# A fused FNet and expert-layer kernel: the slots of its tile pairs in another order, and three late operand sums and four value fills in other places

## The chip, the cores and the metric

The kernel runs on one core of a Trainium2 chip. The metric is the device time of one execution in microseconds (us). A core has a matrix engine (TensorE, PE in the profile, its weight loads PEld), VectorE (DVE), ScalarE (ACT), GpSimd (POOL), and SyncE (SP), which here issues almost all DMA transfers. Every engine works through its own list of instructions in order; semaphores make one engine wait for another.

## The reference

With `x` of 2048 tokens by 512 values, the kernel computes a sum of three things:

```python
xn = layernorm(x)
a, b = xn @ dft_hid_re.T, xn @ dft_hid_im.T
fnet = dft_seq_re @ a - dft_seq_im @ b          # real part of a 2-D Fourier transform

q = xn @ w_q                                    # 32 heads, two halves of 128
s1, s2 = q1 @ k1.T, q2 @ k2.T                   # 64 scores each
top 2 of each -> 4 candidate pairs -> best 2 -> expert i1 * 64 + i2, g = softmax
peer = sum over heads and picks of g * gelu(xn . u[expert]) * v[expert]   # 4096 experts

out = x + fnet + peer
```

## The kernel before

**Precision.** Operands are held as two 16-bit parts, high and low, and a product is three matmuls: high by high, high by low, low by high.

**Stages.** The first 120 us compute the Fourier part. From about 120 to 420 us the routing stage runs: 8 chunks of heads (`j`) by 16 tiles of 128 tokens (`i`). For each of the 128 (j, i) steps, `scores` computes 12 matmuls into a PSUM bank (L252), ACT copies them to an SBUF tile `ss` (L951), and DVE finds the two best values and their places (L955, L959). After a chunk, `routing` turns the picks into experts and gates (L884 to L924): parts on POOL, parts on DVE, one exponential on ACT (L892). The last chunk's routing runs on DVE alone. Into the same 128 steps a table `todo` hangs extra work, one list of functions per step: `fill_load` and `fill_uv` load 512 KB of `u` or `v` and split it (ACT L780 and L781, then POOL L782); `sum_x(b, ...)` forms, for one pair of token tiles, the four sums of operand blocks that the pairs need later (POOL L822 to L831), splits them (ACT L794, POOL L795) and stores them to DRAM (`t_d`, SP L798). `sum_x` and the fills share SBUF: the sums of pair b=8 are formed in the space of `v` tiles 5 and 6, those of b=10 in that of 7 and 8, and those of b=12 again in 5 and 6, so that these four `v` tiles can be filled only when the sums in them are out. These fills are the last four of the list `fills`.

**The dense stage.** From 420 us every token tile is multiplied with all 4096 experts (z), the result goes through a gelu, is multiplied by the gates (a comparison on DVE and matmuls L1252 give them), and is multiplied with `v` (L1297). The order of the phases is z0, z1, v0, then six pairs, each followed by two v phases: z(2,3), v1, v2, z(4,5), v3, v4, and so on up to z(12,13). The pairs begin on PE at 490.6, 577.4, 666.9, 756.2, 844.3 and 933.8 us.

**A pair.** `z_pair` handles two token tiles at once. Half of the 16 expert groups are *plain tiles* (`u_part`, 24 matmuls of 256 columns, L1095, 2.62 us on PE). The other eight form two quads, `a` and `b`; each quad is computed by seven *part products* in place of eight (24 matmuls of 128 columns, L1164, 1.34 us each), from sums of operand blocks. A string `SEQ` sets the order on PE: "1a" is part product 1 of quad a, "c" a plain tile. Part products 1, 2 and 5 of a quad open a PSUM bank each (X, Y, Z); 6, 7 and 4 go on in X, and 3 in Z. After each slot, ACT or DVE takes the intermediate out: 1 and 5 and 6 and 7 by an ACT copy (L1198, L1203, L1205, L1211), 2 and 3 by a DVE addition (L1200, L1208), 7 also by L1212, with gelus (L1191) behind 6, 7 and 4. A plain tile takes one bank and ends in two gelus (L1102). There are four banks for all this, handed out first in, first out; Y is free after 2's addition, Z after 3's, X only after 4's gelu.

**Side work in a pair.** Slots of a pair that use a sum of `u` blocks (5, 6, 3, 7) read it from a ring of three SBUF buffers `s`, 512 KB each. A small planner decides which load goes behind which use (`ring_plan`); SP issues it when that use's matmuls are done (L1147). At fixed shares of the pair's time, `after` adds other units: the gate work, and checks of the Fourier inputs (`compare`), which load a 64 KB and a 448 KB piece (`cx`, L1326, L1327), reduce and subtract on DVE (L1328, L1347, L1353) and sum absolute values on ACT (L1373).

```python
SEQ = "1a 5a 2a c 6a c 3a c 7a c 1b 5b 4a 2b c 6b c 3b 7b c c 4b".split()
for n, b in zip((19, 22, 25, 107, 111, 114), PAIRS):
    todo[n].append(lambda at, b=b: sum_x(b, 0, at))
```

Within each engine the program's final order is set by a scheduler when the kernel is built, so it is not exactly the order of the code.

Of the kernel before, what the change touches and what calls it, by code (L numbers as in the profile page):

```python
# [29 lines left out]
V1 = 5  # L30
V2 = 9
QUADS = (8, 10, 12, 14), (9, 11, 13, 15)
PAIRS = tuple(range(2, 14, 2))
# [3 lines left out]
def tile_fnet_peer(ctx, tc, x, ca, cb, c5, wt, wf, wr, wq, kt, ut, vn, out):  # L37
# [683 lines left out]
    def part_b(safe, stS, stP, stQ, stE, xt, u_sb, cmp_p, w4):  # L721
# [11 lines left out]
        def behind(src, at):  # L733

            if at is None:
                return src
            nc.scalar.activation(at, src, AF.Copy)
            return at
# [48 lines left out]
        def scratch(g):  # L787
            return v_sb[g].rearrange("p l c d -> p (l c d)").bitcast(F32)

        def split4(part, t, h, dst, at):  # L790

            l = t.bitcast(F16)[:, 0:2 * D]
            if part == 0:
                nc.scalar.activation(h, t, AF.Copy, scale=behind(one, at))  # L794
                nc.gpsimd.tensor_tensor(l, t, h, op=ALU.subtract)  # L795
                return
            for i, v in enumerate((h, l)):
                nc.sync.dma_start(dst(i), v)  # L798
# [17 lines left out]
        def sum_x(b, part, at=None):  # L816

            n = (0, 2, 4, 5, 7, 5)[PAIRS.index(b)]
            f, t4 = scratch(n), scratch(n + 1)
            if part == 0:  # L820
                v = xq[b // 2]
                nc.gpsimd.tensor_copy(f[:, 0:1], behind(one, at))  # L822
                nc.gpsimd.tensor_tensor(f.rearrange("p (q f) -> p q f", q=2),  # L823
                                        v[:, :, 0].rearrange("p q k n -> p q (k n)"),
                                        v[:, :, 1].rearrange("p q k n -> p q (k n)"), op=ALU.add)
                b11, b21, b12, b22 = [f[:, k * 256:k * 256 + 256] for k in range(4)]
                r = [t4[:, k * 256:k * 256 + 256] for k in range(4)]
                nc.gpsimd.tensor_tensor(r[0], b12, b11, op=ALU.subtract)
                nc.gpsimd.tensor_tensor(r[1], b22, r[0], op=ALU.subtract)
                nc.gpsimd.tensor_tensor(r[2], b22, b12, op=ALU.subtract)  # L830
                nc.gpsimd.tensor_tensor(r[3], b21, r[1], op=ALU.subtract)  # L831
                return
            split4(part - 1, t4, f.bitcast(F16)[:, 0:2 * D],
                   lambda i: t_d[b // 2, :, i * 2 * D:i * 2 * D + 2 * D], at)
# [132 lines left out]
        todo = [[] for _ in range(NCH * NT)]  # L967
# [8 lines left out]
        else:  # L976
# [8 lines left out]
            for j in range(2, NCH):  # L985
                for t in range(4):
                    todo[(j - 1) * NT + 2 * t - (12 if j == 2 else 4)].append(
                        lambda at, j=j, t=t: m_prep(j, t, wqp, behind(sw, at)))
        fills = [divmod(n, 16) for n in (0, 1, 2, 8, 3, 10, 16, 4, 12, 14, 17, 5, 9, 11, 18, 6, 13, 15, 19, 7, 20,
                                         21, 22, 23, 24)]  # L990
        slots = [29, 31, 36, 43, 45] + [16 * j + i for j in range(3, 7) for i in (4, 6, 11, 13)]
        slots += [119 + 2 * n for n in range(len(fills) - len(slots))]
        assert fills[slots.index(119)] == (1, V1)
        for (which, g), n in zip(fills, slots):
            todo[n].append(lambda at, w=which, g=g: fill_uv(w, g, at))
            todo[n - (3 if n < 119 else 1)].append(lambda at, w=which, g=g: fill_load(w, g))
            if which == 0 and not safe and any(g in q for q in QUADS):
                todo[n + 5].append(lambda at, g=g: (sum_u(g, 1, at), sum_u(g, 2)))
        if not safe:
            for n, b in zip((19, 22, 25, 107, 111, 114), PAIRS):  # L1000
                todo[n].append(lambda at, b=b: sum_x(b, 0, at))
                todo[n + (4 if n == 114 else 5)].append(lambda at, b=b: (sum_x(b, 1, at), sum_x(b, 2)))
        for g, n in zip(range(V2, 16), (25, 38, 41, 57, 73, 89, 105)):
            todo[n].append(lambda at, g=g: stage_v(g, at, False))
            todo[n - 3].append(lambda at, g=g: fill_load(1, g))
# [98 lines left out]
        if not safe:  # L1104
            sx = stE.enter_context(tc.tile_pool(name="sx", bufs=1, side="left"))
            x4 = sx.tile([P, 2, 4, 2, P], F16, name="x4")
            PLAIN = [g for g in range(16) if not any(g in q for q in QUADS)]
            SEQ = "1a 5a 2a c 6a c 3a c 7a c 1b 5b 4a 2b c 6b c 3b 7b c c 4b".split()
            OPS = {"1": (0, None, None, 0), "2": (1, None, None, 1), "5": (None, 0, 0, None), "6": (None, 1, 1, None),
                   "3": (None, 3, None, 3), "7": (None, 2, 2, None), "4": (3, None, 3, None)}  # L1110

        USES = []
        if not safe:
            clock = 0
            for n in range(len(PAIRS)):
                for o in SEQ:
                    ns = 2616 if o == "c" else 1344
# [53 lines left out]
        def z_pair(b, n, after):  # L1171

            cgs = iter(PLAIN)
            st = {}
            total, done, cg = sum(2616 if o == "c" else 1344 for o in SEQ), 0, 0
            for o in SEQ:
                if o == "c":
# [374 lines left out]
        for ph in phases[2:]:  # L1552
            if ph[0] == "z":
                n = 4 * len(ph[1:]) - 2
# [26 lines left out]
        for n, ph in enumerate(phases):  # L1581
            if ph[0] == "z":
                b = ph[1:]
# [13 lines left out]
            b = ph[1]  # L1597
# [23 lines left out]
        return None if safe else ret  # L1621

    rs = part_b(False, stS, stP, stQ, stE, xt, u_sb, cmp_p, w4)
    stR = ExitStack()
    stR.enter_context(tc.If(rs > 0))
    r2 = nc.values_load(flag2, min_val=0, max_val=1)
    with tc.If(r2 > 0):
        MS.clear()
        stE = ExitStack()
        uvp = stE.enter_context(tc.tile_pool(name="uvp2", bufs=1, side="right"))  # L1630
        cmp_p = stE.enter_context(tc.tile_pool(name="cmpp2", bufs=1, side="right"))
        w4 = wq_space("w4p2")
        u_sb = [uvp.tile([P, 2, 2, KD, P], F16, name=f"us{g}") for g in range(16)]
        stQ = ExitStack()
        PS[0] = stQ.enter_context(tc.tile_pool(name="psum2", bufs=1, space=bass.MemoryType.PSUM))
        stP = ExitStack()
        PA[0] = stP.enter_context(tc.tile_pool(name="psa2", bufs=1, space=bass.MemoryType.PSUM))
        stS = ExitStack()
        xtp = stS.enter_context(tc.tile_pool(name="xtp2", bufs=1, side="left"))
        xt = [xb2[:, i] if i < 2 else xtp.tile([P, 2, KD, P], F16, name=f"xs{i}") for i in range(NT)]  # L1640
        for i in range(NT):
            nc.sync.dma_start(xt[i].rearrange("p a k n -> p (a k n)"), xt_d[i])
        for k in range(2):
            MP[k] = stS.enter_context(tc.tile_pool(name=f"mps{k}", bufs=1, side="left"))
        part_b(True, stS, stP, stQ, stE, xt, u_sb, cmp_p, w4)
# [3 lines left out]
    with tc.If(rv > 0):  # L1649
        with tc.tile_pool(name="gen", bufs=1) as gp, \  # L1650
# [22 lines left out]
            for q in range(4):  # L1673
                ya = gp.tile([P, 4, D], F32, tag="ya", name=f"gya{q}")
                for ri in range(2):
# [25 lines left out]
                    for a in range(4):  # L1701
                        py = pb(f"gy{q}{ri}{a}")
                        n = 0
# [9 lines left out]
                        b = 4 * a + q  # L1713
# [55 lines left out]
```

## Time and profile before

| | |
|---|---|
| median of 3 runs | 1145.59 us (1145.26 to 1149.68) |
| the profiled execution | 1145.57 us |
| its span (first to last instruction) | 1143.8 us |
| granted TensorE clock, mean | 0.996 |
| routing stage | about 120 to 420 us |
| six pairs, first to last start | 490.6 to 933.8 us |

A row of the timeline reads: start, duration, engine, line, operation, output<-input, and in brackets how long the engine had been idle and what released it. A row of the waits reads: engine and line that waited, what it waited for, then the sum in us, how often, and the longest.

### The profile page before, as it was taken

The page shows a single profiled execution, that of the slowest core. Times are in us where ns is not written, and L with a number is a line of the kernel's source. Part 1 is how long each engine was busy: PE and PEld are TensorE (multiplying, and loading weights), DVE is VectorE, ACT ScalarE, POOL GpSimd, SP SyncE. Part 2 cuts the span into 40 slices and gives each one's busy share as a digit, 9 for nine tenths or more (in the row PEclk, how much of TensorE's full clock was granted, in tenths as well). Part 3 has the DMA queues.
Part 4 walks back from the last instruction along what each step waited for, and adds up shares of the span by engine and source line. Part 5 has one row for each costly group of instructions (what it writes and reads, how often), then busy time and mean ns, then how long its engine had stood idle before and what let it go on. Part 6 is the DMA issues. An engine that isn't in the chain of part 4 may idle for free.

```text
span 1143.8 us, 27323 instructions
## 1 busy us (share of the span) xinstructions
PE 1123.1 (98%) x10748; PEld 726.1 (63%) x10748; DVE 949.7 (83%) x2855; ACT 642.1 (56%) x1086; POOL 312.3 (27%) x342
## 2 busy tenths in 40 slices
PE   9999999999999999999999999999999999999997
PEld 6455454544544469687487488479478569567763
DVE  7899979989889899956985895895996886889782
ACT  6557598788787374454444445435435534545542
POOL 1415896887888730000000000000010010000000
PEclk8999999999999999999999999999999999999999
DMA  9884455435333216453752762763663654565743
GB/s 283 278 208 162 164 167 188 140 110 194 114 134 105 75 51 207 157 210 123 259 180 101 243 222 92 229 213 119 222 206 131 219 198 145 186 235 174 237 148 105
DMA packets 114856, 198.36 MB, mean 173 GB/s; under 512 B 34068, under 2 KB 57499, under 8 KB 114718
## 3 DMA queue, kind: packets, MB, share of 16 engines
q1 hardware_dynamic: 114416, 196.45, 51.5%
q8 instruction: 86, 1.41, 0.5%
q14 instruction: 52, 0.43, 0.1%
q10 hardware_dynamic: 302, 0.08, 0.1%
HBM read 165.75 MB, written 24.97 MB: 167 GB/s over the span
## 4 chain that ended last, share of the span: by engine, by line
PE 50%; DVE 7%; DMA 5%; POOL 2%; ACT 2%; issue 1%; SPq 0%; ACTq 0%; POOLq 0%; DVEq 0%
PE v L1297 24%; PE z L1095 14%; PE z L1164 7%; DMA cx<-in_cb_dram 4%; PE g L1252 4%; PE s L252 2%; DVE L L1242 1%; DVE w L1260 1%; DVE cx L1347 1%; DVE act L1268 1%; ACT cx L1373 1%; POOL v L823 1%; DMA fit<-in_wq_dram 1%; DVE R L1247 0%; DVE R L1250 0%
## 5 line engine op out<-in xcount | busy, mean ns | idle before, releaser
L252 PE MATMUL s<-m,xq 128*128 128x512 f16 x1344 | 297.4, 379 | 2.5 <-ACT ss L951 2.5
L1297 PE MATMUL v<-v,act 128*128 128x512 f16 x1056 | 233.3, 379 | 0.0
L252 PEld LDWEIGHTS <-xq 128*128 128x128 f16 x1344 | 129.7, 98 | 153.5 <-issue 3.8
L1095 PE MATMUL z<-xb,u 128*128 128x128 f16 (+1 forms) x2688 | 219.9, 242 | 5.0 <-ACT act L1191 4.7
L1095 PEld LDWEIGHTS <-u 128*128 128x128 f16 x2688 | 196.7, 98 | 18.2 <-issue 5.6
L1310 POOL TENSOR_TENSOR y<-y,xr 128x512 f32<-128x512 f32 x15 | 24.6, 1643 | 638.8 <-DMA y<-y_d 380.5
L1242 DVE TENSOR_TENSOR L<-io_lam,cmp 128x2048 f16<-128x2048 f16 x128 | 158.4, 1237 | 41.3 <-PE g L1252 41.3
L1297 PEld LDWEIGHTS <-act 128*128 128x128 f16 x1056 | 101.2, 98 | 117.6 <-issue 0.2
L955 DVE MAX8 vals<-ss 128x8 f32<-128x64 f32 x896 | 133.4, 216 | 3.0 <-ACT ss L951 3.0
L951 ACT ACTIVATE ss<-s,wsc 128x512 f32<-128x512 f32 x120 | 81.7, 684 | 44.1 <-PE s L252 35.5
L1297 PE MATMUL v<-v,w 128*128 128x512 f16 x480 | 106.2, 379 | 0.0
L1373 ACT ACTIVATE cx<-cx 128x896 f32<-128x896 f32 x64 | 60.4, 943 | 63.5 <-DVE cx L1353 49.0
L959 DVE FIND_INDEX8 idx<-vals,ss 128x8 uint16<-128x256 f32 x224 | 93.8, 419 | 0.0
L1267 ACT ACTIVATE act<-w 128x1024 f16<-128x1024 f32 x36 | 48.4, 1360 | 69.2 <-DVE w L1260 69.0
L1297 PEld LDWEIGHTS <-w 128*128 128x128 f16 x480 | 45.9, 98 | 53.4
L1102 ACT ACTIVATE act<-z,scl 128x256 f32<-128x256 f32 (+1 forms) x88 | 44.1, 525 | 49.5 <-PE z L1095 49.5
L1252 PEld LDWEIGHTS <-L 128*128 128x128 f16 x2048 | 60.2, 96 | 12.0 <-issue 1.5
L1260 DVE SCALAR_TENSOR_TENSOR w<-act,scl,g 128x1024 f32<-128x1024 f32 x44 | 55.7, 1276 | 13.4 <-ACT act L1191 13.4
L1347 DVE TENSOR_TENSOR cx<-cx 128x512 f32<-128x512 f32 (+2 forms) x84 | 48.4, 610 | 18.6 <-DMA cx<-in_cb_dram 18.5
L1164 PEld LDWEIGHTS <-s 128*128 128x128 f16 x1080 | 62.7, 98 | 0.5
L1252 PE MATMUL g<-R,L 128*128 128x32 f16 x2048 | 62.0, 176 | 1.0 <-DVE R L1250 0.9
L1268 DVE TENSOR_TENSOR act<-w,act 128x1024 f16<-128x1024 f32 x44 | 59.2, 1348 | 2.3 <-ACT act L1267 2.3
(363 smaller groups left out, 1729.2 us busy)
## 6 DMA issues: line engine op xcount, KB each, us to landing
v<-v_d SPq DMA_DIRECT2D x67, 512.0 KB, 4.6
cx<-in_cb_dram SPq DMA_DIRECT2D x64, 448.0 KB, 5.4
s<-s_d SPq DMA_DIRECT2D x35, 512.0 KB, 4.5
w<-in_wq_dram SPq DMA_DIRECT2D x28, 512.0 KB, 6.1
fit<-in_wq_dram SPq DMA_DIRECT2D x28, 512.0 KB, 4.3
uv<-in_vn_dram SPq DMA_DIRECT2D x16, 512.0 KB, 4.0
uv<-in_ut_dram SPq DMA_DIRECT2D x16, 512.0 KB, 4.0
c<-in_ca_dram SPq DMA_DIRECT2D x8, 512.0 KB, 7.5
```

Of the source, the lines that this page charges most:

```text
L252: nc.tensor.matmul(ps, xt[i][:, l, kd, :], m[:, r, kd, :], start=(n == 0), stop=(n == 3 * KD - 1))
L951: nc.scalar.activation(s, ps, AF.Copy, scale=inv)
L955: nc.vector.max(vals[:, i, w, :, h], s[:, g, :])
L959: nc.vector.max_index(idx[:, i, w].rearrange("p k h -> p (k h)"), vals[:, i, w, 0:2].rearrange("p k h -> p (k h)"), s[:, w * HC:g + 1, :]. ...
L1095: nc.tensor.matmul(ps if n == 1 else ps.rearrange("p (b n) -> p b n", b=2), ug[:, l, c % 2, kd, :], xb2[:, k0, r, kd, :] if n == 1 else xb ...
L1164: nc.tensor.matmul(bank[:, t * P:(t + 1) * P], lt, rt, start=(t == k == 0 and op in "125"), stop=(t == 3 and k == 5), skip_group_check=op ...
L1242: nc.vector.tensor_tensor(L.rearrange("p t (l two) -> p t l two", two=2), io_lam.rearrange("p (l two) -> p l two", two=2).unsqueeze(1).to_ ...
L1252: nc.tensor.matmul(p[:, hf, t * NC:(t + 1) * NC], L[:, t, :], R[:, t, :], start=True, stop=True)
L1260: nc.vector.scalar_tensor_tensor(w, act[:, :, ts], fw, p.rearrange("p h (n c) -> p c (h n)", c=NC), op0=ALU.mult, op1=ALU.mult)
L1268: nc.vector.tensor_tensor(w16[..., 1], w, w16[..., 0], op=ALU.subtract)
L1297: nc.tensor.matmul(pv, w16[:, c, :, l], v_sb[g][:, r, cc, :], start=(n + cc == 0 and k == 0), stop=(n == 15 and cc == 1 and k == 2))
L1373: later.append(lambda: nc.scalar.activation(tf[:, P:], tf[:, P:], AF.Abs, accum_out=chk[:, n:n + 1]))
```

## The change

Three tables change; the numbers of instructions on every engine stay as they were.

```diff
         fills = [divmod(n, 16) for n in (0, 1, 2, 8, 3, 10, 16, 4, 12, 14, 17, 5, 9, 11, 18, 6, 13, 15, 19, 7, 20,
-                                         21, 22, 23, 24)]
+                                         23, 24, 21, 22)]
         slots = [29, 31, 36, 43, 45] + [16 * j + i for j in range(3, 7) for i in (4, 6, 11, 13)]
-        slots += [119 + 2 * n for n in range(len(fills) - len(slots))]
-        assert fills[slots.index(119)] == (1, V1)
+        slots += [119 + 2 * n for n in range(4)]
...
-            for n, b in zip((19, 22, 25, 107, 111, 114), PAIRS):
+            for n, b in zip((19, 22, 25, 106, 109, 118), PAIRS):
                 todo[n].append(lambda at, b=b: sum_x(b, 0, at))
-                todo[n + (4 if n == 114 else 5)].append(lambda at, b=b: (sum_x(b, 1, at), sum_x(b, 2)))
+                todo[n + (4 if n == 118 else 5)].append(lambda at, b=b: (sum_x(b, 1, at), sum_x(b, 2)))
...
-            SEQ = "1a 5a 2a c 6a c 3a c 7a c 1b 5b 4a 2b c 6b c 3b 7b c c 4b".split()
+            SEQ = "1a 5a 2a c 6a c 3a c 1b 7a 2b 5b 6b 4a c 3b c c 7b c c 4b".split()
```

The last four fills (numbers 21 to 24 are `v` tiles 5 to 8, at steps 119, 121, 123, 125) come as 7, 8, 5, 6 instead of 5, 6, 7, 8. The sums for pairs b=8, 10, 12 start at steps 106, 109, 118 instead of 107, 111, 114. In a pair the first eight slots stay; then six part products stand in a row (1b 7a 2b 5b 6b 4a), and the two plain tiles that stood among them come later. One line less in the code moves all later line numbers down by one: L1164 of before is L1163 in the change.

On POOL, at the end of the routing stage's chunk 6 (its routing ends in L924, L895, L924), this is one piece of the difference; `c`, `z`, `g`, `lc`, `di` belong to `routing`; `v_920` and `v_921` are the space of `v` tiles 5 and 6, `v_922` and `v_923` that of 7 and 8:

```order
-L795 TENSOR_TENSOR v_921<-v_921,v_920 128x1024
 L924 CAST z<-lc_0_5210 128x16x2x4 x2
+L895 TENSOR_TENSOR g_0_5272<-c_0_5163,g_0_5272 128x16x4
+L795 TENSOR_TENSOR v_923<-v_923,v_922 128x1024
 L924 CAST z<-di_0_5202 128x16x2x4 x2
-L822 COPY v_920<-ss_2_5185 128x1
+L822 COPY v_920<-ss_6_5328 128x1
 L823 TENSOR_TENSOR v_920<-xq_109 128x1024
 L828 TENSOR_TENSOR v_921<-v_920 128x256
```

The sum block of pair b=12 (L822 on) stood ahead of the gate multiplication L895 of chunk 6, and now stands behind it.

On DVE, in the middle of pair b=4 (`cx` are compare tiles; L1212, in the change L1211, is the addition behind 7a; L1200, in the change L1199, the addition behind 2b), before:

```order
L1328 TENSOR_REDUCE sums<-cx_8897 128x1
L1347 TENSOR_TENSOR cx_8897<-cx_8897 128x768
L1212 TENSOR_TENSOR w_126<-w_126,act_8248 128x4x128
L1353 TENSOR_TENSOR cx_8897<-cx_8897 128x128
L1328 TENSOR_REDUCE sums<-cx_8984 128x1
L1347 TENSOR_TENSOR cx_8984<-cx_8984 128x768
L1353 TENSOR_TENSOR cx_8984<-cx_8984 128x128
L1200 TENSOR_TENSOR act_8248<-z_4_0_8651,act_8248 128x4x128
```

and with the change:

```order
L1327 TENSOR_REDUCE sums<-cx_8897 128x1
L1346 TENSOR_TENSOR cx_8897<-cx_8897 128x768
L1327 TENSOR_REDUCE sums<-cx_8984 128x1
L1352 TENSOR_TENSOR cx_8897<-cx_8897 128x128
L1211 TENSOR_TENSOR w_126<-w_126,act_8248 128x4x128
L1346 TENSOR_TENSOR cx_8984<-cx_8984 128x768
L1199 TENSOR_TENSOR act_8248<-z_4_0_8563,act_8248 128x4x128
L1352 TENSOR_TENSOR cx_8984<-cx_8984 128x128
```

The addition behind 2b still has both compare subtractions (128x768) ahead of it, and has moved ahead of one short one.

On ACT, at the same place in pair b=4 (L1373 is the compare's absolute sum; L1198, L1203, L1205, L1211 the copies behind 1b, 5b, 6b, 7a; L1191 on `z_4_1_8249` the gelu behind 4a, which frees that bank), before:

```order
L1373 ACTIVATE cx_8897,sums<-cx_8897 128x896
L1102 ACTIVATE act_8248<-z_3_8537,scl 128x256
L1102 ACTIVATE w_126<-z_3_8537,scl 128x256
L1373 ACTIVATE cx_8984,sums<-cx_8984 128x896
L1198 ACTIVATE act_8248<-z_4_0_8568 128x4x128
L1203 ACTIVATE act_8248<-z_4_0_8594 128x4x128
L1191 ACTIVATE act_8248<-z_4_1_8249,scl 128x4x128
```

and with the change (each line number one less):

```order
L1197 ACTIVATE act_8248<-z_4_0_8508 128x4x128
L1210 ACTIVATE w_126<-z_4_1_8249 128x4x128
L1372 ACTIVATE cx_8897,sums<-cx_8897 128x896
L1190 ACTIVATE w_126<-w_126,scl 128x4x128
L1190 ACTIVATE act_8248<-act_8248,scl 128x4x128
L1202 ACTIVATE act_8248<-z_4_0_8593 128x4x128
L1372 ACTIVATE cx_8984,sums<-cx_8984 128x896
L1204 ACTIVATE w_126<-z_4_0_8508 128x4x128
L1190 ACTIVATE act_8248<-z_4_1_8249,scl 128x4x128
```

The copy behind 1b now precedes both absolute sums; the gelu behind 4a still follows both. The gelu on `act_8248` alone takes the result of 2b's addition.

## The prediction

> **What bounds the kernel now.** I read the page first, then what PE waited for, then idle time by stage, and at each place with a wait the chain of waits and the timeline.
>
> ```profile
> PE 1123.1 (98%) x10748; PEld 726.1 (63%) x10748; DVE 949.7 (83%) x2855; ACT 642.1 (56%) x1086; POOL 312.3 (27%) x342
> ```
>
> PE is busy for 98% of the 1143.8 us span, and the change takes no instruction from it. So only PE's idle time can be saved. Its waits over the whole run, the longest first (waits at other lines, of 1.0 us or less each line, are left out):
>
> ```profile
> PE z L1095 <- ACT act L1191: 4.7, 4, 1.8
> PE s L252 <- ACT ss L951: 2.5, 1, 2.5
> ...
> PE z L1164 <- ACT act L1102: 0.5, 1, 0.5
> PE z L1164 <- ACT w L1102: 0.5, 1, 0.5
> ```
>
> Two groups stand out: one wait of 2.5 us in the routing stage (L252), and waits of 4.7 + 0.5 + 0.5 = 5.7 us at matmuls of the pairs (L1095 and L1164). No row names a DMA behind a pair's matmul. The busy time in windows places them, each from the start of a pair to the start of the next (columns: window, its length, then PE, PEld, DVE, ACT, POOL busy, clock, DMA share, GB/s):
>
> ```profile
> 490.60:577.40 86.80, 86.80 (x946) 61.92 (x945) 64.25 (x128) 40.01 (x69) 2.80 (x2) 1.00 0.50 178
> 577.40:666.90 89.50, 88.05 (x984) 62.84 (x981) 68.63 (x108) 40.68 (x70) 3.25 (x2) 1.00 0.55 186
> 666.90:756.20 89.30, 87.79 (x979) 62.70 (x976) 69.36 (x108) 40.98 (x70) 4.72 (x2) 1.00 0.55 186
> 756.20:844.30 88.10, 87.78 (x981) 62.80 (x978) 71.58 (x124) 41.33 (x70) 3.03 (x2) 1.00 0.56 188
> 844.30:933.80 89.50, 87.75 (x984) 62.83 (x981) 73.79 (x130) 40.95 (x70) 3.19 (x2) 1.00 0.55 186
> 933.80:1024.00 90.20, 89.11 (x1005) 64.04 (x1002) 70.67 (x120) 43.33 (x76) 3.63 (x2) 1.00 0.53 183
> ```
>
> Length less PE's busy time: 0 in pair b=2, then 1.45, 1.51, 0.32, 1.75 and 1.09 us. The sum is 6.1: the waits' 5.7, and small ones. The clock is 1.00 everywhere, so it plays no part.
>
> **Why PE waits in a pair.** Pair b=4 in the timeline, PE alone:
>
> ```profile
> 592.74 1.50 PE L1164 MATMUL z<-x,s 128*128 128x128 f16 x24
> ...
> 601.35 1.50 PE L1164 MATMUL z<-xb,u 128*128 128x128 f16 x24 [0.47 <-ACT w L1102]
> ...
> 603.83 2.78 PE L1095 MATMUL z<-xb,u 128*128 128x256 f16 x24 [0.98 <-ACT act L1191]
> ```
>
> These are 7a, then 2b, which stands right behind 4a, and the plain tile behind 2b. The plain tile needs 4a's bank, and only 2b's 1.34 us lie between them. The chain of waits says why ACT is late with it:
>
> ```profile
> 585.52 0.79 PE g L1252 x32
> 586.31 2.63 PE z L1095 x24
> 588.94 1.35 PE z L1164 x24
> ...
> 590.69 6.61 DMA cx<-in_cb_dram
> ...
> 597.32 0.96 DVE cx L1347
> 598.28 0.61 DVE w L1212
> ...
> 601.19 1.03 ACT cx L1373 x2
> ...
> 602.71 0.49 ACT act L1203
> 603.20 0.59 ACT act L1191
> ```
>
> A compare tile takes 6.61 us to land. The absolute sums of it and of the tile behind it (1.03 us each; the chain's row is the second) then stand on ACT's list ahead of the plain gelu (for 2b's bank), of two copies, and of 4a's gelu.
>
> **The pairs after the change.** I call T the start of 1b, where 7a began (592.74 in pair b=4; the slots ahead of it stay). With the 1.34 us of a part product (1.35 above), 2.63 of a plain tile and 0.8 of 32 gate matmuls, PE runs 7a at T+1.34, 2b at 2.68, 5b at 4.02, 6b at 5.36, 4a at 6.70, a plain tile at 8.04, 3b at 11.45, and plain tiles at 12.80 and 15.4. The bank that 4a frees is now needed by the plain tile at T+12.80 = 605.54, 4.8 us behind 4a's end, where it was 1.34.
>
> What is late next? The plain tile at T+8.04 = 600.78 takes 2b's bank, free after DVE's addition (L1200). On DVE's list it stands behind compare work: the first subtraction, then 7a's addition with a short reduction and a short mirror, the second subtraction, and itself.
>
> ```profile
> 599.20 0.95 DVE L1347 TENSOR_TENSOR cx<-cx 128x768 f32<-128x768 f32 x1
> ...
> 602.95 0.69 DVE L1200 TENSOR_TENSOR act<-z,act 128x512 f32<-128x512 f32 x1 [2.48 <-PE z L1164]
> ```
>
> The first subtraction ends at 597.32 + 0.96 = 598.28, and from there to the second, at 599.20, the three small ones took 0.92. So the addition ends 0.92 + 0.95 + 0.69 = 2.56 later, at 600.84: a new wait of 0.1 us, with the semaphore. Then ACT, which takes five steps behind this addition (gelu 0.59, copy 0.49, absolute sum 1.03, copy 0.49, 4a's gelu 0.59, together 3.2), has freed 4a's bank at 604.0, 1.5 ahead of its need. In pair b=6 the first subtraction comes a little later against T:
>
> ```profile
> 682.15 1.50 PE L1164 MATMUL z<-x,s 128*128 128x128 f16 x24
> ...
> 686.79 0.96 DVE L1347 TENSOR_TENSOR cx<-cx 128x768 f32<-128x768 f32 x1 [1.90 <-DMA cx<-in_cb_dram]
> ```
>
> 686.79 + 0.96 + 2.56 = 690.31 against 682.15 + 8.04 = 690.19, so 0.15 us. In b=8, 10 and 12 I have not followed each step to a tenth, and set 0.15 us each. **Pairs: 6.1 - (0.1 + 4 x 0.15) = 5.4 us saved.** The bounds: the new waits cost nothing (6.1 saved), or one more subtraction comes ahead of the addition in each of the five pairs (0.96 each, 4.8 more, 0.6 saved). I stay near the first end, because the order of DVE's list shows just two.
>
> The Trainium skill (Perfetto Trace Analysis, Optimization Strategy) says that a gap repeating on the engine that should be full can mean too little SBUF or PSUM for the next tile. By that rule a new order would only shift the gap to another of the four banks, and the sum would keep the pairs' 6.1 us. This trace agrees in part: the wait is for a bank, but pair b=2, with as many banks and no compare tile in its way, shows none.
>
> **Ring loads.** Their number stays, and SP issues them at the same places of its list, for other uses. The tightest is now the load behind 6a, needed by 7a at T+1.34 = 594.08:
>
> ```profile
> 586.65 0.43 SPq L1147 DMA_DIRECT2D s<-s_d  x1
> ...
> DMA to landing us min/median/max: 3.2/4.5/5.9
> ```
>
> 594.08 - 586.65 = 7.4 us for a landing of at most 5.9. In pair b=2, where SP is held by another wait, the load was issued late:
>
> ```profile
> 501.34 10.98 SPq L1147 DMA_DIRECT2D s<-s_d  x4
> ...
> 505.17 1.50 PE L1164 MATMUL z<-x,s 128*128 128x128 f16 x24
> ```
>
> It has 505.17 + 1.34 - 501.34 = 5.2 us, above the median 4.5 but below the maximum. I count it as nothing; the bound is 0.7 us there.
>
> **The routing stage.** The 2.5 us wait, followed back:
>
> ```profile
> 388.15 2.13 POOL L823 TENSOR_TENSOR v<-xq 128x1024 f32<-128x1024 f16 x1
> ...
> 393.21 0.32 POOL L895 TENSOR_TENSOR g<-c,g 128x64 f32<-128x64 f32 x1
> ...
> 393.57 2.13 DVE L896 CAST z<-g 128x128 f16<-128x128 f32 x1 [2.38 <-POOL g L895]
> ...
> 400.72 0.21 ACT L892 ACTIVATE c<-c 128x16 f32<-128x16 f32 x1 [10.90 <-DVE c L889]
> ...
> 401.56 18.41 PE L252 MATMUL s<-m,xq 128*128 128x512 f16 x84 [2.46 <-ACT ss L951]
> ```
>
> The sum block of pair b=12 (from 388.15, one long operation and four shorter ones) stands ahead of L895. DVE waits 2.38 us for it, comes late to the last chunk's first routing (L889), ACT's exponential (L892) waits for that in front of the score copies, and PE runs out of banks. The change puts the block behind L895: DVE's wait of 2.38 us goes, and L895 no longer follows the block, so I let PE's 2.46 us go whole. What is late next: `sum_x` of b=12 and the fills of tiles 5 and 6 now run at the end of the stage. Before:
>
> ```profile
> 401.63 1.15 ACT L794 ACTIVATE v<-v,ss 128x1024 f16<-128x1024 f32 x1
> 402.81 2.59 SPq L798 DMA_DIRECT2D t_d<-v  x2
> 402.92 2.13 POOL L795 TENSOR_TENSOR v<-v,v 128x1024 f16<-128x1024 f32 x1 [7.31 <-ACT v L794]
> 405.08 1.15 ACT L780 ACTIVATE v<-uv,ss 128x1024 f16<-128x1024 f32 x1 [1.64 <-POOL v L795]
> ```
>
> The split and store from 401.63 to the end of the issues (405.4) took 3.8 us, and ACT stood 1.64 us for it at the fill of tile 5, without PE noticing. In the change the split comes four steps later in the table, but the stage runs 2.46 us earlier, so about 403 + 3.8 + a landing put that fill at 408 to 409. Its two ACT operations of 1.15 us stand ahead of a score copy at about 411, which PE needs about 4 us later (an estimate from 2.65 us of PE per tile: 12 matmuls of 18.41/84). I set that at nothing; the bound is the old wait, 2.46. **Routing: 2.46 us saved, bounds 0 and 2.46.**
>
> **Sum.** The profiled execution took 1145.57 us (1.8 of it outside the span), the median is 1145.59: no correction. 1145.57 - 5.4 - 2.46 = 1137.7. The phases behind the pairs are full on PE, so the gains pass to the end. **Forecast 1137.7 us, 0.7% faster.** I call 0.5% (5.7 us) what a measurement of this kernel can tell from no change.
>
> **Rivals.**
> 1. *The pairs' wait moves* to the plain tile at T+8.04. For it: the same compares are still ahead of the bank's release, and the bound above, or the whole 6.1 us if every gap returns. Against it: 4a's bank gets 3.4 us more time. Only the routing pays: 1145.57 - 2.46 - 0.6 = 1142.5, or 1143.1 with nothing saved (the skill's rule comes to that too). Within 0.5%. Chance 0.17.
> 2. *The routing wait stays*, with ACT held by the fill of tile 5 or 6 until the sums are stored. For it: the 1.64 us above. Against it: about 4 us of room. 1145.57 - 5.4 = 1140.2, within 0.5%. Chance 0.11.
> 3. *Ring loads come late* (the slower side). The six part products in a row read three ring buffers in 5.4 us, and the loads lie beside compare tiles that take 6.61. Against it: 5.9 at most, room 7.4. It decides from a landing of 7.4 us on; at twice the median, 9.0, 7a waits 1.6 us, and later loads with some 8 us of room 1.0 twice. Up to 3.6 us in each of six pairs is 21.6: 1145.57 - 2.46 - 5.4 + 21.6 = 1159.3; with the first alone (9.6), 1147.3. Between them 1153. Chance 0.12.
> 4. *The change does not do what it says*: the compares land elsewhere and all waits stay, 1145.6. Chance 0.05.
>
> **Numbers.** The forecast has 0.55 (its own range 1137.0, with all 6.1 and 2.46 saved, to 1139.8). Faster by over 0.5% (under 1139.9) is the forecast and a fourth of rival 2 that ends just there: 0.58. Same: the rest of rival 2, rivals 1 and 4, a quarter of rival 3: 0.33. Slower: 0.09. The range 1136.2 to 1146.0 reaches from the full gain, less a little scatter, over rivals 1, 2 and 4; outside lie rival 3 and a few hundredths.
>
> **What would show it.** Right: the wait at L252 gone or under 0.3 us; L895 ahead of the sum block on POOL; in pairs b=4 and b=6 no wait behind 4a, and a wait of 0.1 to 0.4 us on L1199 (L1200 before) at the plain tile behind it; PE idle in the five windows under 1.5 us together. Wrong: a DMA of `s` behind a pair's matmul (rival 3), waits on L1199 near 1 us (rival 1), a wait at L252 late in the stage (rival 2), all old waits in their old places (rival 4), or DVE work of the checks pushed into the end of the program, where PE no longer covers it.

## The result, and the profile after

| | before | changed |
|---|---|---|
| median of 6 runs each | 1146.02 us (1144.47 to 1149.68) | 1135.95 us (1134.83 to 1138.71) |
| ratio, 95% interval | | 0.991 (0.9892 to 0.9928) |
| the profiled execution, its span | 1145.57, 1143.8 | 1134.83, 1133.0 |

The change made the kernel 10.1 us (0.9%) faster. The forecast was 1137.7 us, with a range from 1136.2: the direction and the main mechanism held, and the gain was a quarter larger than forecast, 0.25 us outside the range.

What PE waited for over the whole run, after the change (all rows from 0.3 us on, but for three more ahead of the score matmuls):

```profile
PE p L449 <- issue: 1.3, 1, 1.3
PE p L449 <- DVE q L419: 1.1, 1, 1.1
...
PE g L1251 <- DVE R L1249: 1.0, 3, 0.5
...
PE s L252 <- DVE m L227: 0.3, 1, 0.3
```

No row is left at the pairs' matmuls (L1094 and L1163 now), and the 2.5 us at L252 are gone. The windows from the start of pair b=4 to the next pair, and so on (columns as above):

```profile
573.62:661.19 87.57, 87.57 (x983) 62.70 (x980) 66.98 (x107) 40.84 (x70) 2.76 (x2) 1.00 0.55 190
661.19:748.75 87.56, 87.56 (x983) 62.71 (x979) 68.48 (x109) 41.03 (x70) 4.28 (x2) 1.00 0.56 189
748.75:836.32 87.57, 87.57 (x984) 62.70 (x980) 72.05 (x125) 41.10 (x70) 3.64 (x2) 1.00 0.56 190
836.32:923.88 87.56, 87.56 (x983) 62.71 (x979) 72.63 (x130) 41.05 (x70) 3.20 (x2) 1.00 0.55 190
923.88:1013.30 89.42, 89.28 (x1010) 64.33 (x1007) 71.66 (x121) 43.36 (x76) 3.60 (x2) 1.00 0.54 186
```

PE is busy in every hundredth of the first four. All four take 87.57 us, which is a pair and its two v phases without any stall. That gives a measure that needs no wait row: what a pair takes over 87.57 us is what its stalls cost.

Where the time went, by stage, from the starts of PE's instructions in the two profiled executions:

| stage on PE | before | changed | saved |
|---|---|---|---|
| start to the score matmul (L252) at 77.39 us | 77.39 | 76.37 | 1.02 |
| from there to the dense stage (z0) | 342.42 | 339.68 | 2.74 |
| z0 to pair b=4 | 157.57 | 157.57 | 0.00 |
| pair b=4 and its v phases | 89.41 | 87.57 | 1.84 |
| pair b=6 | 89.39 | 87.56 | 1.83 |
| pair b=8 | 88.16 | 87.57 | 0.59 |
| pair b=10 | 89.47 | 87.56 | 1.91 |
| pair b=12 to the end | 209.95 | 209.15 | 0.80 |

The score matmul that parts the first two rows is not the first one: 96 others run from 23.7 us on, among the Fourier part. It stands at the same place of PE's list in every kernel here, and the routing stage is counted from it in what follows.

The sum is 10.7, the difference of the spans but for rounding. Its first row is no work of the change: nothing is changed there, and over all kernels of this document the same stretch took between 75.15 and 79.07 us. The granted clock in the first 25 us (column ahead of the DMA share) differed, before:

```profile
0.00:25.00 25.00, 23.16 (x130) 17.49 (x131) 17.21 (x54) 15.41 (x32) 3.93 (x20) 0.86 0.93 278
```

and after:

```profile
0.00:25.00 25.00, 22.03 (x137) 16.38 (x138) 18.23 (x57) 16.97 (x37) 3.56 (x20) 1.00 0.92 277
```

Without that row the two profiles differ by 9.7 us, close to the 10.1 of the medians: 2.74 in the routing stage and 6.97 in the pairs and behind them. The last row is the least certain: in the kernels with the new order it took between 207.90 (the last experiment) and 209.66 us.

Pair b=4 after the change (T = 588.98 is the start of 1b; the rows are the second and third compare subtraction, 2b's addition, the plain tile that takes its bank, 4a's gelu, and the two plain tiles behind 3b, merged in one row that the end of the view cuts off):

```profile
592.65 0.96 DVE L1346 TENSOR_TENSOR cx<-cx 128x768 f32<-128x768 f32 x1 [0.81 <-DMA cx<-in_cb_dram]
...
594.53 0.95 DVE L1346 TENSOR_TENSOR cx<-cx 128x768 f32<-128x768 f32 x1
...
595.39 0.68 DVE L1199 TENSOR_TENSOR act<-z,act 128x512 f32<-128x512 f32 x1
...
597.02 2.78 PE L1094 MATMUL z<-xb,u 128*128 128x256 f16 x24
...
598.63 0.69 ACT L1190 ACTIVATE act<-z,scl 128x512 f32<-128x512 f32 x1
...
601.78 4.42 PE L1094 MATMUL z<-xb,u 128*128 128x256 f16 x39
```

4a's bank is free at 599.3, 2.5 us ahead of its need. 2b's addition ends at 596.1, 0.9 us ahead of its need, where a wait of 0.1 was forecast: the compare tile landed earlier against T (its subtraction starts at T+3.67, before at T+4.58). In pair b=12, where T is 939.24, it did not, and the subtraction starts at T+4.73:

```profile
943.97 1.03 DVE L1346 TENSOR_TENSOR cx<-cx 128x256 f32<-128x256 f32 x2 [2.19 <-DMA cx<-in_cb_dram]
...
945.91 1.02 DVE L1346 TENSOR_TENSOR cx<-cx 128x256 f32<-128x256 f32 x2
...
946.85 0.68 DVE L1199 TENSOR_TENSOR act<-z,act 128x512 f32<-128x512 f32 x1
947.58 2.78 PE L1094 MATMUL z<-xb,u 128*128 128x256 f16 x24
```

There the plain tile starts at T+8.34 instead of T+8.04. This is the forecast new wait; it came once, in one of five pairs.

### The profile page after: what moved, and what is told of

Its sections match the earlier page's. It is cut to its first block, busy times and chain, and to the rows that moved or that the text cites. A ratio compares the mean times of both kernels' runs of the same rounds, so it can differ in the third digit from the quotient of the medians.

```text
span 1133.0 us, 27318 instructions
## 1 busy us (share of the span) xinstructions
PE 1118.9 (99%) x10748; PEld 724.0 (64%) x10748; DVE 943.8 (83%) x2855; ACT 641.1 (57%) x1086; POOL 312.6 (28%) x342
## 4 chain that ended last, share of the span: by engine, by line
PE 83%; DVE 10%; DMA 4%; ACT 1%; issue 1%; SPq 0%; POOL 0%; DVEq 0%; ACTq 0%
PE s L252 27%; PE v L1296 24%; PE z L1094 17%; PE z L1163 9%; PE g L1251 4%; DMA cx<-in_cb_dram 2%; PE m L148 1%; DVE u L955 1%; DVE L L1241 1%; DVE u L959 1%; DVE w L1259 1%; PE p L449 1%; DVE cx L1346 1%; DVE act L1267 1%; DMA xq<-u 1%
## 5 line engine op out<-in xcount | busy, mean ns | idle before, releaser
L252 PE MATMUL s<-m,xq 128*128 128x512 f16 x1344 | 297.1, 379 | 0.3 <-DVE m L227 0.3
L252 PEld LDWEIGHTS <-xq 128*128 128x128 f16 x1344 | 129.8, 98 | 151.2 <-issue 1.2
L1094 PE MATMUL z<-xb,u 128*128 128x128 f16 (+1 forms) x2688 | 219.0, 242 | 0.1
L1094 PEld LDWEIGHTS <-u 128*128 128x128 f16 x2688 | 196.7, 98 | 13.1 <-issue 0.3
L955 DVE MAX8 vals<-ss 128x8 f32<-128x64 f32 x896 | 133.4, 216 | 2.4 <-ACT ss L951 2.4
L1163 PEld LDWEIGHTS <-s 128*128 128x128 f16 x1080 | 62.4, 98 | 0.4
```

The costliest lines, as they stand in the source:

```text
L252: nc.tensor.matmul(ps, xt[i][:, l, kd, :], m[:, r, kd, :], start=(n == 0), stop=(n == 3 * KD - 1))
L955: nc.vector.max(vals[:, i, w, :, h], s[:, g, :])
L1094: nc.tensor.matmul(ps if n == 1 else ps.rearrange("p (b n) -> p b n", b=2), ug[:, l, c % 2, kd, :], xb2[:, k0, r, kd, :] if n == 1 else xb ...
L1163: nc.tensor.matmul(bank[:, t * P:(t + 1) * P], lt, rt, start=(t == k == 0 and op in "125"), stop=(t == 3 and k == 5), skip_group_check=op ...
```

## Experiments

All build on one of the two kernels. For each, the starts on PE give two numbers: the routing stage (from the score matmul named above to z0; 342.42 before, 339.68 changed) and what the pairs b=4 to b=10 take over 87.57 us.

### The two halves alone

The pairs' order alone, in the kernel before:

```diff
-SEQ = "1a 5a 2a c 6a c 3a c 7a c 1b 5b 4a 2b c 6b c 3b 7b c c 4b".split()
+SEQ = "1a 5a 2a c 6a c 3a c 1b 7a 2b 5b 6b 4a c 3b c c 7b c c 4b".split()
```

> Only the order of the pairs' slots is changed, the routing tables stay. Theory A (the pairs' waits go by themselves, and each stall costs about 0.16 us more than its idle time shows, because the last matmul before it drains): the pairs b=4 to b=12 take together 6.5 to 7.5 us less, every one about 87.6 us from start to start, no wait at L1095 above 0.4 us; the wait of 2.5 us at L252 stays. Time 7 us below before. Theory B (the earlier end of the routing stage helped the pairs, DVE coming to them with less left over): over 1.5 us of waits come back in the pairs, time 4 to 5 us below before.

Median 1139.47 us of 12 runs, ratio 0.995 (0.993 to 0.9969). The routing stage took 342.41 us, with its wait:

```profile
PE s L252 <- ACT ss L951: 2.4, 1, 2.4
```

The pairs took 87.63, 87.56, 87.79 and 87.56 us (b=2, untouched by the old waits, 0.5 us more than before, with a wait for gate work). Theory A holds: the pairs' waits go by themselves.

The routing tables alone (the fills and the sums of x moved as in the change, the old `SEQ`):

> Only the sums of x and the last four fills of v are moved, the pairs keep the old order of slots. Theory A: the dense stage starts 2.6 us earlier against the start of the routing stage (2.46 of wait and 0.16 of drain), the pairs' waits come back at about 6 us, and the time is 2.5 to 3 us below before. Theory B: the pairs' waits come back smaller (under 4.5 us), and the time is over 4 us below before.

Median 1144.26 us of 12 runs, ratio 0.9981 (0.9959 to 1.0002), which alone tells little. The stages tell more: the routing stage took 339.69 us, and the pairs 89.55, 88.91, 88.74 and 91.25, together 8.2 us over 4 x 87.57. The waits came back, larger than in the profiled execution of before (6.15 over). So each half does its own work, though the time of this one came out 1.8 us below before (1146.10 in the same series), less than theory A's 2.5 to 3. The stalls of the old order are no fixed sum: in the five kernels here that have it they took 5.5 to 9.0 us, one profiled execution each.

### What made DVE late in the routing stage

The prediction put the 2.46 us down to L895, which stood behind the sum block of b=12 on POOL. If that is all, taking L895 off POOL must do it:

```diff
-ge.tensor_tensor(g[:, :, 1, :], ex, g[:, :, 0, :], op=ALU.mult)
+nc.vector.tensor_tensor(g[:, :, 1, :], ex, g[:, :, 0, :], op=ALU.mult)
```

> The kernel before, with the gate multiplication L895 on DVE instead of POOL in all chunks; the sum block of pair b=12 stays where it is on POOL. Theory A (DVE waited because L895 stood behind the sum block): DVE's wait of 2.4 us goes, L252's wait of 2.46 us falls under 0.5 us, time 2.5 us below before. Theory B (what made DVE late were its conversions of 2.13 us, each beside POOL's L795, 1.9 us too long): L252 still waits over 1 us, time within 1.5 us of before.

The wait fell only to 1.89 us, the stage took 341.88 us, and the median was 1145.52 us (ratio 0.9989, 0.9966 to 1.0013). By the numbers this is theory B. But the edit moves L895 in all chunks, and DVE came 1.9 us late to the end of chunk 6, so the small gain does not show that the wait for L895 counted little; the table of waits below takes this up. The timeline of this run, at the end of chunk 6, shows another cause of lateness:

```profile
384.55 2.13 POOL L795 TENSOR_TENSOR v<-v,v 128x1024 f16<-128x1024 f32 x1
384.63 2.13 DVE L918 SCALAR_TENSOR_TENSOR di<-c,i2s 128x64 int32<-128x64 f32 x1 [0.51 <-POOL i2s L914]
```

L918 is 64 values per partition. It ended with POOL's L795, which had started 0.08 us ahead of it. The changed kernel has L918 and L896 apart from it, but another DVE instruction, L921, still meets L795 there:

```profile
385.11 0.22 DVE L918 SCALAR_TENSOR_TENSOR di<-c,i2s 128x64 int32<-128x64 f32 x1
...
386.20 0.32 POOL L895 TENSOR_TENSOR g<-c,g 128x64 f32<-128x64 f32 x1
386.48 2.13 POOL L795 TENSOR_TENSOR v<-v,v 128x1024 f16<-128x1024 f32 x1
...
386.97 0.47 DVE L955 MAX8 vals<-ss 128x8 f32<-128x64 f32 x3
387.35 1.35 DVE L921 TENSOR_SCALAR di<-di 128x128 int32<-128x128 int32 x1
...
389.02 0.20 DVE L896 CAST z<-g 128x128 f16<-128x128 f32 x1
...
394.25 0.17 DVE L889 TENSOR_TENSOR c<-c,c 128x16 f32<-128x16 f32 x1
```

L918 takes 0.22 us and L896 0.20, against 2.13 each before. Each of the two collisions makes a DVE instruction 1.9 us longer, nearly as much as the wait for L895 (2.38) that the prediction built on. The next three runs move one block or operation each. First, only the block of b=12 moved, in the changed kernel:

```diff
-            for n, b in zip((19, 22, 25, 106, 109, 118), PAIRS):
+            for n, b in zip((19, 22, 25, 107, 111, 118), PAIRS):
```

> The changed kernel with the sums of b=8 and b=10 back at steps 107 and 111; only the sums of b=12 are moved (118). Theory A (moving the block of b=12 behind L895 is what counts): no wait at L252 over 0.5 us, time within 0.7 us of the changed kernel. Theory B (the earlier two blocks, which keep POOL's L795 away from DVE's conversions, count as well): L252 waits 1 us or more, and the time is 1 to 2.5 us above the changed kernel.

Median 1137.86 us of 10 runs (ratio 0.9929, 0.9908 to 0.9949). Both collisions were there:

```profile
383.46 2.13 POOL L795 TENSOR_TENSOR v<-v,v 128x1024 f16<-128x1024 f32 x1
383.54 2.13 DVE L918 SCALAR_TENSOR_TENSOR di<-c,i2s 128x64 int32<-128x64 f32 x1 [0.50 <-POOL i2s L914]
...
390.74 2.13 POOL L795 TENSOR_TENSOR v<-v,v 128x1024 f16<-128x1024 f32 x1
390.81 2.13 DVE L896 CAST z<-g 128x128 f16<-128x128 f32 x1 [0.50 <-POOL g L895]
```

The wait of 2.46 was gone with both collisions in place, as theory A says. One of 0.57 stood at a later place of L252 (410.18 us), where the score copy stands on ACT's list behind the two operations of a fill; so L252's wait lies between the two theories, and the time, 1.9 us above the changed kernel by the medians, is theory B's. The stage took 340.84 us, 1.58 of the 2.74 us saved. Then only the blocks of b=8 and b=10, in the kernel before:

```diff
-            for n, b in zip((19, 22, 25, 107, 111, 114), PAIRS):
+            for n, b in zip((19, 22, 25, 106, 109, 114), PAIRS):
```

> The kernel before with only the sums of b=8 and b=10 moved (106 and 109); b=12 stays at 114, so its long addition L823 still stands ahead of L895 on POOL. Theory A (PE waits because L889 comes later than about 320.6 us after the start of the score matmuls, and DVE's two collisions with POOL's L795 count as much as the wait for L895): with one collision less L889 comes 2 to 4 us earlier, the wait at L252 is under 0.5 us. Theory B (the block of b=12 must be moved): L252 waits 1.5 us or more.

Theory A by its numbers: no wait at L252 for the score copies, the stage took 339.84 us (one run, 1142.23 us). The block of b=12 keeps its step. But its four shorter operations now stand behind L895 in POOL's list, and DVE no longer waits for L895. Last, the second part of one block, with its POOL operation L795, the ACT copy and the stores:

```diff
-                todo[n + (4 if n == 114 else 5)].append(lambda at, b=b: (sum_x(b, 1, at), sum_x(b, 2)))
+                todo[n + {114: 4, 107: 3, 111: 5}.get(n, 5)].append(lambda at, b=b: (sum_x(b, 1, at), sum_x(b, 2)))
```

> The kernel before with one thing moved: the second part of the sums of b=8 (its L795 on POOL) comes two steps earlier, so that it no longer runs beside DVE's L918 in chunk 6. The block of b=12 keeps its step, and its long L823 stays ahead of L895 on POOL. Theory A (PE waits as far as L889 comes later than about 320.6 us after the start of the score matmuls, and DVE is held until POOL's long operation ends when the two collide): L918 takes 0.2 us in place of 2.13, L889 comes about 320 us after the start or earlier, the wait at L252 is under 0.3 us. Theory B (L895 behind the block's long operation is what costs the 2.46 us): the wait at L252 stays at 1.5 us or more.

```profile
386.14 0.22 DVE L918 SCALAR_TENSOR_TENSOR di<-c,i2s 128x64 int32<-128x64 f32 x1
...
387.43 2.12 POOL L823 TENSOR_TENSOR v<-xq 128x1024 f32<-128x1024 f16 x1
389.51 0.31 POOL L895 TENSOR_TENSOR g<-c,g 128x64 f32<-128x64 f32 x1
389.79 0.72 POOL L828 TENSOR_TENSOR v<-v 128x256 f32<-128x256 f32 x1
...
396.05 0.17 DVE L889 TENSOR_TENSOR c<-c,c 128x16 f32<-128x16 f32 x1
```

The block's long L823 stands ahead of L895, as before, and the wait is gone all the same: 339.74 us for the stage (one run, 1143.24 us). This does not refute the prediction's cause, though: the block's four shorter operations (L828 and on, 0.72 us each) stood ahead of L895 before and stand behind it here, as in the run before this one, and L895 runs 3.7 us earlier against the stage. Eight kernels in one order, by the start of L889 after that score matmul:

| kernel | L889 | routing stage |
|---|---|---|
| order of slots alone | 323.07 | 342.41 |
| before | 323.06 | 342.42 |
| L895 on DVE | 322.58 | 341.88 |
| block of b=12 alone | 320.30 | 340.84 (other wait, 0.57) |
| blocks of b=8 and b=10 | 319.79 | 339.84 |
| one subtraction earlier | 318.67 | 339.74 |
| routing tables alone | 317.86 | 339.69 |
| changed | 317.88 | 339.68 |

PE waits here by as much as L889 comes later than about 320.6 us (323.06 - 2.46; 322.58 - 1.89 gives 320.7). It came 5.2 us earlier with the change, twice what was needed.

What made DVE late can be added up from its rows. The table starts at one and the same instruction in each kernel, the 70th MAX8 (L955) ahead of L889. It shows how long DVE waited for POOL before L887 and before L896, how much longer than usual L918 and the pair L896 and L897 took, and the whole time to L889:

| kernel | wait before L887 | wait before L896 | L918 too long | L896, L897 too long | whole time |
|---|---|---|---|---|---|
| before | 1.10 | 2.38 | 1.91 | 1.93 | 30.87 |
| L895 on DVE | 0.58 | none | 1.91 | 1.78 | 28.50 |
| block of b=12 alone | 1.13 | 0.50 | 1.92 | 1.93 | 27.98 |
| blocks of b=8 and b=10 | 3.15 | none | none | 1.83 | 27.43 |
| one subtraction earlier | 3.14 | none | none | 0.87 | 26.43 |
| changed | 3.17 | none | none | none | 25.70 |

That MAX8 starts 292.2 to 292.4 us after the score matmul in all of them but the second, where it starts at 294.1. From there on L895 on DVE saved 2.37 us, not 0.54. The wait before L896 is 0.50 us or none in every other kernel of this table. Moving the block of b=12 alone brings L889 2.76 us earlier, more than the 2.46 that PE waited. The collision of L918 was not all gain: where it is gone, L795 stands ahead of L884 on POOL, and DVE waits for that instead, before:

```profile
380.32 0.22 DVE L887 TENSOR_TENSOR pm<-c,c 128x64 f32<-128x64 f32 x1 [1.10 <-POOL c L886]
```

and with the change:

```profile
378.36 2.13 POOL L795 TENSOR_TENSOR v<-v,v 128x1024 f16<-128x1024 f32 x1
...
381.35 0.22 DVE L887 TENSOR_TENSOR pm<-c,c 128x64 f32<-128x64 f32 x1 [3.17 <-POOL c L886]
```

With two shorter waits, before L916 and L918, that went as well (0.86 us together), parting L918 from L795 was worth about 0.7 us, and parting L896 from it 1.9.

### What the order of the slots does

The changed kernel with 4a's bank needed 1.34 us after it again, but with the plain tiles still late:

```diff
-SEQ = "1a 5a 2a c 6a c 3a c 1b 7a 2b 5b 6b 4a c 3b c c 7b c c 4b".split()
+SEQ = "1a 5a 2a c 6a c 3a c 1b 7a 5b 4a 2b c 6b 3b c c 7b c c 4b".split()
```

> The changed kernel with the order 1b 7a 5b 4a 2b c 6b 3b c c 7b c c 4b behind the eighth slot: the plain tiles stand late as in the change, but the bank that 4a frees is needed again 1.34 us after 4a, by the plain tile behind 2b. Theory A (what counts is how long after 4a its bank is needed): PE waits come back at that plain tile, 1 us or more in most of the pairs b=4 to b=12, together 5 us or more. Theory B (what counts is that plain tiles no longer stand between part products): all pairs stay at 87.6 us from start to start.

```profile
PE z L1094 <- ACT act L1190: 5.9, 4, 2.2
PE z L1163 <- ACT w L1210: 2.8, 2, 1.5
...
PE z L1094 <- ACT w L1190: 1.6, 1, 1.6
```

One run of 1150.33 us. The waits on 4a's gelu came back (5.9 + 1.6), and 4a itself now waited for 7a's copy (L1210), only one slot ahead of it. Theory A: with the short distance to the bank's next use the waits are back, though the plain tiles stand late. The opposite case, 4a early and the plain tiles in their old places:

```diff
-SEQ = "1a 5a 2a c 6a c 3a c 1b 7a 2b 5b 6b 4a c 3b c c 7b c c 4b".split()
+SEQ = "1a 5a 2a c 6a c 3a c 7a c 4a 1b 5b 2b c 6b c 3b 7b c c 4b".split()
```

> The changed kernel with the old places of the plain tiles and 4a moved ahead of 1b (c 7a c 4a 1b 5b 2b c 6b c 3b 7b c c 4b), so that its bank is needed 4 us after it. Theory A: the waits on 4a's gelu (4.7 us in all before) fall under 1 us together; the waits of 2b on a plain tile's gelu (0.5 us in some pairs) may stay, pairs at 87.6 to 88.3 us. Theory B: the waits on 4a's gelu come back, 4 us or more together.

Of the pairs' waits one row is left:

```profile
PE z L1163 <- ACT w L1210: 0.5, 1, 0.5
```

The pairs took 88.17, 87.63, 87.90 and 87.56 us, 1.0 us over in all (one run, 1137.48 us). Moving 4a alone brings most of the gain; the row of six part products is not what does it.

Last, 3b ahead of the plain tile behind 4a, for the 0.3 us of b=12:

```diff
-SEQ = "1a 5a 2a c 6a c 3a c 1b 7a 2b 5b 6b 4a c 3b c c 7b c c 4b".split()
+SEQ = "1a 5a 2a c 6a c 3a c 1b 7a 2b 5b 6b 4a 3b c c c 7b c c 4b".split()
```

> The changed kernel with 3b ahead of the plain tile behind 4a, so that 2b's addition has 1.34 us more before its bank is needed. Theory A (the small waits left in single pairs, 0.3 us in b=12 of the changed kernel, are 2b's addition behind the compare subtractions on DVE): all pairs at 87.56 us, tail 0.3 us shorter, time within 0.5 us of the changed kernel. Theory B: a new wait of 3b for the copy behind 5b on ACT, 0.3 us or more in some pairs.

```profile
PE z L1163 <- ACT act L1202: 4.2, 4, 2.4
```

Theory B: 3b waits for the copy behind 5b, which stands on ACT's list behind 2b's addition. Median 1140.17 us of 10 runs, ratio 0.995 (0.9929 to 0.997), where the changed kernel has 0.991 (0.9892 to 0.9928). The plain tile there covers this copy.

## Why the prediction was right or wrong

**PE sets the time, and only its idle time can go:** right. In the two parts that the change touches, the 9.7 us saved are, but for some tenths, stalls and what a stall costs beside its idle time (below); 98% busy became 99%.

**4a's bank needed too soon, behind the compares on ACT:** right, and shown by the slots put back (waits of 7.5 us on 4a's gelu) and by 4a moved alone.

**The term of the pairs, "6.1 - (0.1 + 4 x 0.15) = 5.4 us saved":** mis-sized, and this is the larger part of the error. It measured 6.97. Two things were wrong in it. First, the new wait behind 4a was charged in all five pairs; it came in one, with 0.3 us, and in b=4, where 0.1 was worked out, the compare tile was issued at the same place as before (2.05 us ahead of T) but landed 0.9 us sooner, which is luck. Second, the idle time of a stall is not its whole cost. Before, the four pairs b=4 to b=10 were idle 1.45 + 1.51 + 0.32 + 1.75 = 5.03 us by the windows, but took 6.15 us over 4 x 87.57. The rows of the prediction held the reason: 24 matmuls are shown as 1.50 us, while the next 24 start 1.34 us later. The 0.16 us that the last one still drains is hidden when work follows, and counts as busy when none does. (The ends of matmul rows are modelled in the profile; what is measured is the distance of the starts.) A single small stall shows it alone, here pair b=8 of the run with only the block of b=12 moved:

```profile
751.42:839.35 87.93, 87.72 (x983) 62.81 (x980) 70.85 (x124) 41.31 (x70) 3.79 (x2) 1.00 0.57 189
```

It was idle 0.21 us and took 0.36 too long, 0.15 more than its idle time. In the pairs of before the differences are 0.39, 0.32, 0.27 and 0.16. Pairs b=4 and b=6 had two waits each and pair b=10 one, at 0.16 a wait; of pair b=8, with one wait, 0.11 is left over, and 0.07 of b=4.

**The routing term, 2.46:** 2.74 measured, 0.16 of it again the drain. The step "the change puts the block behind L895: DVE's wait of 2.38 us goes" held: the block of b=12 moved alone brings L889 2.76 us earlier, and the wait of PE that the step names is gone there. What the step lacked is DVE held by POOL's long operations. L896 with its 2.13 us was quoted in the prediction, and its length was not asked about. The changed kernel, which moves the other two blocks as well, has L889 another 2.4 us earlier. PE did not need that at this place, but with the block alone it waits 0.57 us later in the stage. So the term came near its size in part by luck: with the block of b=12 alone, the only cause that it names, the stage saves 1.58 us.

**The fills of tiles 5 and 6 at the stage's end:** no wait, as forecast.

**Rivals.** Ring loads did not come late: no row names them in any run (rows of four runs name loads of `v`, 0.2 to 0.8 us). The pairs' wait did not move, but in one pair. The routing wait did not stay.

**The base.** The prediction added its terms to an execution at 1145.57, near the median shown then; with three more runs that median is 1146.02. Together: 6.97 for 5.4 and 2.74 for 2.46 make 9.7 us, where 7.9 were forecast.

## What to carry to other kernels

Banks handed out first in, first out make the distance between the slot that frees a bank and its next use the quantity to plan: count it in time, and count what stands on the freeing engine's list in between. Put the cost of a stall at its idle time plus what the last instruction drains, and check it against an equal stage without stalls. When a short VectorE instruction shows ten times its usual duration, look what GpSimd does at that moment before explaining the wait in front of it, and after the two are parted, look whether the time has only become a wait elsewhere.

## What the hardware showed that I had not expected

Some DVE instructions were held until POOL's operation ended, not merely slowed. Before, the conversion L896 (128 values of a partition, one input) took 2.13 us when it met L795, and 0.20 us in the changed kernel beside a short POOL conversion; two more rows from the kernel before show the ends together:

```profile
383.33 2.13 POOL L795 TENSOR_TENSOR v<-v,v 128x1024 f16<-128x1024 f32 x1
383.40 2.13 DVE L918 SCALAR_TENSOR_TENSOR di<-c,i2s 128x64 int32<-128x64 f32 x1 [0.51 <-POOL i2s L914]
```

Where L896 came in the middle of a POOL operation, in five chunks before, it took 1.28 to 1.34 us and ended with it. It is no rule for every instruction: the MAX8 (L955) took 0.21 to 0.22 us in all 234 cases of the kernel before in which it ran beside L795, L823 or L782, as long as elsewhere, and in the first chunk L896 took 0.21 us beside L823. The Trainium skill (GPSIMD Engine Reference, Specifications) says that POOL shares its SBUF interface with DVE, contending with DVE instructions in a 2-port mode or with two SBUF inputs. That agrees with L918, which has two inputs; L896 has one, and no run here shows which mode it ran in.
